# A banded convolution in windows of three quarters, with lent PSUM banks and shared copies, in front of a token-mixing kernel

## The chip, the cores and the metric

The kernel runs on one core of a Trainium2 chip. The metric is the device time in microseconds of one execution; a run's time is compared by the median of several. A profiled execution gives a trace of every instruction, with its span from the first instruction to the last.

## What is computed

The input `x` has 8 batches, 4224 tokens and 192 channels. A causal convolution with 7 taps runs over the tokens, with softmaxed weights per head (8 heads of 24 channels). Its result goes through a token mixing with phases. Cut to what matters:

```python
out = np.einsum('hk,bskhg->bshg', softmax(weight), windows_of_7(x))   # convolution
x = out
theta = x @ w_theta
zr, zi = x * np.cos(theta), x * np.sin(theta)
y = np.einsum('ts,bsd->btd', w_tok_r, zr) + np.einsum('ts,bsd->btd', w_tok_i, zi)
u = x + y
return u + np.maximum(u @ w_ch, 0.0)
```

The token mixing is by far the largest part: two 4224 x 4224 matrices, each against 8 x 192 columns.

## The kernel before

**Tiling.** The source tokens are cut into 33 chunks (`NCH`) of 128 tokens. A chunk is not contiguous: it has four quarters of 32 tokens (`NQ`, `Q`), one from each quarter of the sequence, and `tokens(c, a)` gives the first token of quarter `a`. The target tokens are cut into 17 units of two blocks of 128 tokens, of which the last has one block. A pair of blocks is done with seven products in place of eight (a Strassen-like scheme with the sums S1 to S4 of weight blocks and T1 to T4 of operands), each in two halves of the columns: 14 matmuls of 384 columns for each chunk and unit, at line 659.

**Visits.** A visit takes one unit through all chunks that are in SBUF at that time, at most 11 (`SLOTS`). `FIRST` says at which visit each of the first 11 chunks enters; every later chunk enters 17 visits after the chunk whose slot it takes. So the first visit works with one chunk, the second with two, and so on to eleven; at the end the number falls again. Between the visits to a unit its partial sums go to DRAM (`part`) and come back. Three of the smallest late visits are moved forward (`extra`), with small tiles of their own.

**A chunk's preparation** (`Chunk`, `prepare`). Each quarter of x is loaded to a buffer `xw` (cast to bf16 on the way), with its 16 history rows: for chunk 0 from DRAM, for the others by a DMA from the chunk before's `xw` (line 265, on SP). The convolution is a matmul with a band matrix `bands` as its stationary side: two quarters of 48 rows (96 rows) at a time, two accumulating matmuls for each head, 16 for each chunk (line 403). Two heads share a PSUM bank, and ScalarE copies each bank to `xz` (line 411). From there the chunk is stored to DRAM (`xs`, for the residual), and transposed: by TensorE with a VectorE copy to `uT` (line 443) for the first 11 chunks, by DMA for the later ones. Channel matmuls with `wth` (line 452) give angles, VectorE clamps them (line 320), ScalarE takes sines (line 348), and VectorE multiplies (line 357) and makes the T operands (line 369) in the chunk's slot tiles r0, i0, r1, i1, t1, t2, t4.

**Weights.** For each visit POOL issues loads of the two token matrices to `st` (line 485). VectorE transposes them in 32 x 32 blocks (line 507) and makes the sums S (line 521).

**PSUM.** Of eight banks, 0 to 5 take the products ("x", "y" and "s", two each). Only banks 6 and 7 serve convolution, transposes and channel matmuls. A product bank's partial result is copied by ScalarE to another bank (line 731) or starts a sum `d` (line 684), or is added to `d` by VectorE (line 686).

**Order.** Every instruction of the main part is a `Step`, with the engine, an assumed duration, its predecessors and the landing time of its DMA. A planner (`Schedule`) simulates the five engines with these assumptions, and issues each engine's instructions in the order that comes out: each engine and each DMA queue then follows this fixed order on the chip. `START` says when each engine is free after the set-up, `LAND` how long DMAs take.

**Set-up.** Before the planned part, POOL makes 0/1 masks, VectorE builds the band matrices (lines 857 to 873), and TensorE runs 18 matmuls on zeros (line 881) that use the identity as their stationary side.

Of the kernel before, what the change touches and what calls it, by code (L numbers as in the profile page):

```python
# [16 lines left out]
def kernel(  # L17
# [22 lines left out]
    nc = tc.nc  # L40
# [9 lines left out]
    HALO = 16  # L50
    WR = Q + HALO
    NT = S // P
    HN = N // 2
# [4 lines left out]
    FIRST = (0, 1, 2, 3, 4, 5, 6, 7, 8, 9, 10)  # L58
    CLAMP = 1.5
    EXTRA = 3  # L60
    BY_PE = 4
    SMALL = 3
# [73 lines left out]
    def pair(u):  # L136
        return 2 * u + 1 < NT


    def pair(u):  # L140
        return 2 * u + 1 < NT


# [22 lines left out]
    class Step:  # L166
        def __init__(self, engine, us, run, after=(), lands=0.0, wire=0.0, frees=None, mm=False):
            self.engine, self.us, self.run = engine, us, run
            self.after, self.lands, self.wire = list(after), lands, wire
            self.frees, self.mm = frees, mm  # L170
            self.due, self.want, self.fixed, self.end = None, None, None, None
            self.number = len(steps)
            steps.append(self)

# [20 lines left out]

    bands = constp.tile([2 * WR, 2 * H + 1, 2, Q], BF16, name="bands")
    nc.vector.memset(bands, 0.0)


    def channel_weights(w, name, after=()):  # L200
        R = D - P
        made = {}

        def clear():
            made["t"] = t = wk.tile([P, 4, D], BF16, name=name, tag="wc", bufs=1)
            dve(nc.vector.memset(t[:, 1:3, :], 0.0))

        ready = [Step("dve", 0.25, clear, after)]
        for lo, hi, k, r0, r1 in ((0, P, 0, 0, P), (0, R, 1, P, D), (R, P, 2, 0, R), (0, P, 3, R, D)):
            ready.append(Step(  # L210
                "pool", 0.6, lambda lo=lo, hi=hi, k=k, r0=r0, r1=r1: pool(nc.gpsimd.dma_start(
                    out=made["t"][lo:hi, k, :], in_=w[r0:r1, :]
                )), ready[:1], lands=4.0, wire=0.3,
            ))
        return (lambda: made["t"]), ready

    xw = tiles(wk, 2, [2 * WR, 2, B, D], BF16, "xw")
    rings = {k: Ring(2) for k in ("xw", "xz", "uT", "ang", "xr", "st", "x", "y", "s")}
# [4 lines left out]
    def load_x(c, a, n, lo, t0, h, k):  # L223
        pool(nc.gpsimd.dma_start(  # L224
            out=xw[k][lo : lo + n, h, :, :],
            in_=x[:, t0 : t0 + n, :].rearrange("b s d -> s b d"),
        ))


    class Chunk:  # L230
        def __init__(self, c):
            self.c, self.early = c, c < SLOTS
            self.k, self.uses, prev = rings["xw"].take()
            self.loads = []
            for a in range(NQ):
                h, lo = a // 2, (a % 2) * WR
                t0 = tokens(c, a)
                if c or t0 == 0:
                    lo += HALO
                else:  # L240
                    t0 -= HALO
                n = (a % 2 + 1) * WR - lo
                args = (c, a, n, lo, t0, h, self.k)
                if c == 0:
                    if t0 == 0:
                        nc.vector.memset(xw[0][0:HALO, 0, :, :], 0.0)
                    load_x(*args)
                    s = Step("none", 0.0, None)
                    s.fixed = START["x0"]
                else:  # L250
                    s = Step(
                        "pool", 0.6, lambda args=args: load_x(*args), [prev],
                        lands=LAND["x"], wire=0.87,
                    )
                self.loads.append(s)
            self.uses += self.loads
            chunks[c] = self
            xwk = xw[self.k]
            self.filled = list(self.loads)
            if c:  # L260
                before = chunks[c - 1]

                def history(a):
                    h, lo = a // 2, (a % 2) * WR
                    sp(nc.sync.dma_start(
                        out=xwk[lo : lo + HALO, h, :, :],
                        in_=xw[before.k][lo + Q : lo + Q + HALO, h, :, :],
                    ))

                for a in range(NQ):  # L270
                    s = Step(
                        "sp", 0.6, lambda a=a: history(a), [before.loads, prev],
                        lands=LAND["history"], wire=0.15,
                    )
                    before.uses.append(s)
                    self.filled.append(s)
            self.uses += self.filled[NQ:]

        def prepare(self):
            c = self.c  # L280
            zk, self.xzuse, prev = rings["xz"].take()
            self.xz = xzt[zk]
            copies = []
            for hp in range(H // 2):
                m = Step("pe", 0.34, lambda b, hp=hp: self.conv(b, hp), [self.filled, bands_ready, prev], mm=True)
                self.uses.append(m)
                e = Step(
                    "act", 0.5, lambda b, hp=hp: self.conv_copy(b, hp), [m], frees=m
                )
                copies.append(e)  # L290
            self.xzuse += copies
            self.xf = self.xz[:, :, :].rearrange("p b d -> p (b d)")
            if c + 2 < NCH:
                Chunk(c + 2)
# [8 lines left out]
            for g in range(2):  # L303
# [3 lines left out]
                turned = transposed(src, uT, [copies, prev], self.early, "sp")  # L307
# [4 lines left out]
                for k2 in range(2):  # L312
# [3 lines left out]
                    )  # L316
                    uuse.append(m)
# [80 lines left out]
        def conv(self, b, hp):  # L398
            for hh in range(2):
                h = 2 * hp + hh  # L400
                for half in range(2):
                    at = 2 * h + 1 - half
                    pe(nc.tensor.matmul(  # L403
                        banks[b][:, hh * B * G : (hh + 1) * B * G],
                        lhsT=bands[:, at : at + 2, :, :].rearrange("p z a m -> p (z a m)"),
                        rhs=xw[self.k][:, half, :, h * G : (h + 1) * G],
                        start=(half == 0), stop=(half == 1),
                    ))

        def conv_copy(self, b, hp):  # L410
            act(nc.scalar.activation(  # L411
                out=self.xz[:, :, hp * 2 * G : (hp + 1) * 2 * G].rearrange(
                    "p b (h g) -> p h b g", h=2
                ),
                in_=banks[b][:, 0 : 2 * B * G].rearrange("p (h b g) -> p h b g", h=2, b=B),
                func=AT.Copy,
            ))

# [7 lines left out]
    def transposed(u, uT, after, by_pe, queue):  # L426
# [8 lines left out]
        def turn(b):  # L435
# [7 lines left out]
        e = Step("dve", 0.55, lambda b: dve(nc.vector.tensor_copy(  # L443
            out=got(uT).rearrange("p k s -> p (k s)"),
            in_=banks[b][:, :].bitcast(BF16)[:, 0 : 6 * P],
        )), [m], frees=m)
# [19 lines left out]
    class Weights:  # L466
# [89 lines left out]
        def tile(self, name):  # L556
            t = self.tiles[name]
            return small_tile()[:, t] if self.small else t
# [7 lines left out]
    def freed_xw():  # L566
        return [s for u in rings["xw"].uses[-2:] for s in u]


    def small_tile():  # L570
        big_tile()
        if "small" not in late:
            late["small"] = wk.tile([P, 7, SMALL, NQ, Q], BF16, name="small", tag="xw")
        return late["small"]

    def big_tile():
        if "big" not in late:
            late["big"] = wk.tile([P, 2, HN], F32, name="late", tag="xw")
        return late["big"]
# [5 lines left out]
    def container(k):  # L585
        if ("u", k) not in late:
            if k < 4:
                both = wk.tile([P, 2, HN], BF16, name="ubT", tag=("ang", "xz")[k % 2])
# [10 lines left out]
    class Visit:  # L599
# [79 lines left out]
        def add(self, q, bank, g, after, begins=False, ends=False):  # L679
            def run():  # L680
                o = self.d[q]()[:, g * PC : (g + 1) * PC]
                y = banks[bank][:, 0:PC]
                if self.first and begins:
                    act(nc.scalar.activation(out=o, in_=y, func=AT.Copy))  # L684
                else:
                    dve(nc.vector.tensor_tensor(out=o, in0=y, in1=o, op=ALU.add))  # L686

            if self.first and begins:
                s = Step("act", 0.49, run, [after, self.start[q]])
# [14 lines left out]
        def products(self):  # L704
# [4 lines left out]
            for r in "xys" if self.pair else "xy":  # L709
                for g in gs:  # L710
                    k, uses[r, g], prev[r, g] = rings[r].take()
                    rows[r, g] = 2 * "xys".index(r) + k

# [15 lines left out]
            def copy(g):  # L729
                kx, ky = rows["x", g], rows["y", g]  # L730
                s = Step("act", 0.48, lambda: act(nc.scalar.activation(  # L731
                    out=banks[ky][:, 0:PC], in_=banks[kx][:, 0:PC], func=AT.Copy
                )), [at["x", g], prev["y", g]])
# [39 lines left out]
        def output(self, q):  # L773
            k, use, prev = outring.take()
            if len(outring.uses) <= 5:
                prev = [
                    s for r in ("ang", "xz", "uT") for u in rings[r].uses[-2:] for s in u
# [37 lines left out]
    START = {"x0": 8.0, "pe": 12.3, "dve": 12.3, "act": 6.3, "pool": 6.6, "sp": 2.0}  # L815
    LAND = {
        "x": 9.0, "history": 6.0, "keep": 6.0, "turn": 11.0, "w": 8.0, "d": 7.5, "store": 5.5,
        "xr": 7.0, "out": 5.0,
    }
    EARLY, SLACK = {}, 12.0  # L820
    noise = wk.tile([P, 512], BF16, name="noise", tag="ang")
    nc.vector.memset(noise, 0.0)
    Chunk(0)
    masks = wk.tile([2 * WR, KS, 2, Q], BF16, name="masks", tag="ang")
# [240 lines left out]
```

## Time and profile before

| | before |
|---|---|
| median of 10 runs | 1443.54 us (1438.73 to 1454.54) |
| the profiled execution | 1442.13 us |
| its span, first instruction to last | 1440.1 us |
| TensorE busy, share of the span | 98% |
| VectorE busy | 77% |
| ScalarE busy | 23% |
| GpSimd (POOL) busy | 36% |
| mean granted TensorE clock | 0.996 |

The time of an execution is 2 us longer than its span. Lines in the profile stand for source lines of the kernel. Busy times of TensorE are modelled from pipelined instructions, so the duration of one matmul in a group overlaps with the next; the distance between two is read from the chain of waits.

### The profile page before, as it was taken

What the parts mean: (1) busy time and instruction counts of PE and PEld (TensorE: products, weight loads), DVE (VectorE), ACT (ScalarE), POOL (GpSimd) and SP (SyncE); (2) the same over time, 40 slices, a digit from 0 to 9 for tenths busy, and PEclk for the clock granted to TensorE, in tenths of its full rate; (3) what the DMA queues carried; (4) which work ended last, traced back from release to release, by engine and by line L of the source; (5) the groups of instructions that cost most, each with busy time, mean ns of one, the idle gap of its engine ahead of it and who ended that gap; (6) DMA issues with size and microseconds to landing.
All of it is one profiled execution on the core that took longest, in us unless ns stands there. A gap on an engine that the chain in (4) does not pass through costs nothing.

```text
span 1440.1 us, 24960 instructions
## 1 busy us (share of the span) xinstructions
PE 1408.6 (98%) x9486; PEld 895.5 (62%) x9486; DVE 1102.8 (77%) x1835; ACT 335.7 (23%) x582; POOL 513.4 (36%) x778
## 2 busy tenths in 40 slices
PE   6899999999999999999999999999999999999997
PEld 3666666666666666666666666666666665666665
DVE  7998764446778987885576888788886878787788
ACT  5764422122212212210000221222121211211221
POOL 7543321124234552133134445225553354411120
PEclk8999999999999999999999999999999999999999
DMA  9999883679999999988799999999995999999994
GB/s 131 257 222 209 155 164 93 123 132 239 198 222 228 253 238 215 223 205 198 183 203 191 234 251 236 220 217 221 248 267 116 212 267 217 237 233 215 237 226 154
DMA packets 341351, 298.44 MB, mean 207 GB/s; under 512 B 160784, under 2 KB 287760, under 8 KB 341232
## 3 DMA queue, kind: packets, MB, share of 16 engines
q0 software_dynamic: 171072, 97.81, 50.6%
q1 hardware_dynamic: 130160, 189.21, 42.7%
q10 hardware_dynamic: 40000, 9.84, 5.4%
q8 instruction: 74, 1.21, 0.3%
q14 instruction: 45, 0.37, 0.1%
HBM read 250.21 MB, written 106.56 MB: 248 GB/s over the span
## 4 chain that ended last, share of the span: by engine, by line
PE 89%; DMA 4%; DVE 2%; issue 1%; ACT 1%; DVEq 0%; SPq 0%; ACTq 0%
PE bank L659 81%; PE bank L452 5%; DMA ubT<-ubT 4%; PE bank L403 3%; PE bank L438 1%; DVE d L686 1%; DVE w L521 0%; DVE d L799 0%; DVE w L507 0%; DMA xw<-xw 0%; DVE ubT L443 0%; ACT ubT L780 0%; DVE uT L443 0%; DVE ang L320 0%; ACT i L348 0%
## 5 line engine op out<-in xcount | busy, mean ns | idle before, releaser
L659 PEld LDWEIGHTS <-w 128*128 128x128 bf16 x7572 | 736.6, 98 | 466.4 <-issue 5.2
L659 PE MATMUL bank<-t,w 128*128 128x384 bf16 x3198 | 558.4, 327 | 1.6 <-DVE w L521 1.4
L686 DVE TENSOR_TENSOR d<-bank,d 128x384 f32<-128x384 f32 x542 | 291.6, 548 | 185.3 <-PE bank L659 156.7
L659 PE MATMUL bank<-i,w 128*128 128x384 bf16 x2220 | 396.3, 327 | 1.0 <-ACT bank L731 0.7
L507 DVE STREAM_TRANSPOSE w<-st 128x640 bf16<-128x640 bf16 (+5 forms) x416 | 340.4, 846 | 70.1 <-PE bank L659 63.0
L659 PE MATMUL bank<-r,w 128*128 128x384 bf16 x2154 | 384.1, 326 | 1.4 <-DVE r L357 1.2
L485 POOL DMA_DIRECT2D st<-in_moe_w_tok_r_dram x244 | 139.9, 582 | 400.7 <-DVE w L507 348.1
L485 POOL DMA_DIRECT2D st<-in_moe_w_tok_i_dram x244 | 139.3, 579 | 150.6 <-DVE w L507 139.5
L521 DVE TENSOR_TENSOR w<-w 128x1408 bf16<-128x1408 bf16 (+10 forms) x220 | 178.2, 810 | 2.5
L631 POOL TENSOR_TENSOR d<-d,xr 128x768 f32<-128x768 f32 x62 | 107.9, 1741 | 147.6 <-DMA xr<-xs 103.0
L224 POOL DMA_DIRECT2D xw<-in_x_dram x132 | 76.4, 588 | 154.9 <-PE bank L403 129.7
L348 ACT ACTIVATE r<-ang,half_pi 128x768 bf16<-128x768 f32 x44 | 41.1, 933 | 311.3 <-DVE ang L320 311.2
L731 ACT ACTIVATE bank<-bank 128x384 f32<-128x384 f32 x116 | 55.0, 477 | 215.8 <-PE bank L659 195.4
L684 ACT ACTIVATE d<-bank 128x384 f32<-128x384 f32 x132 | 63.3, 491 | 160.3 <-PE bank L659 158.6
L411 ACT ACTIVATE xz<-bank 128x384 bf16<-128x384 f32 x132 | 60.4, 489 | 168.4 <-issue 115.4
L320 DVE TENSOR_SCALAR ang<-bank 128x384 f32<-128x384 f32 x132 | 68.7, 550 | 25.8 <-PE bank L452 25.1
L799 DVE SCALAR_TENSOR_TENSOR d<-bank,d 128x384 f32<-128x384 f32 x106 | 55.3, 550 | 20.1 <-PE bank L452 19.5
L780 ACT ACTIVATE ubT<-d 128x768 bf16<-128x768 f32 x44 | 36.8, 842 | 144.5 <-DVE d L686 114.9
L452 PEld LDWEIGHTS <-uT 128*128 128x128 bf16 x632 | 55.6, 98 | 18.4 <-issue 3.4
L403 PE MATMUL bank<-xw,bands 96*128 96x192 bf16 x528 | 60.0, 247 | 2.0 <-ACT xz L411 1.1
L452 PE MATMUL bank<-wth,uT 128*128 128x192 bf16 x528 | 59.1, 249 | 2.6 <-DMA wth<-in_moe_w_theta_dram 1.7
L403 PEld LDWEIGHTS <-bands 96*128 96x128 bf16 x528 | 46.9, 98 | 15.4 <-issue 3.8
(68 smaller groups left out, 551.0 us busy)
## 6 DMA issues: line engine op xcount, KB each, us to landing
part<-d SPq DMA_DIRECT2D x172, 384.0 KB, 4.3
d<-part SPq DMA_DIRECT2D x159, 384.0 KB, 5.3
st<-in_moe_w_tok_r_dram POOLq DMA_DIRECT2D x152, 176.0 KB, 6.4
st<-in_moe_w_tok_i_dram POOLq DMA_DIRECT2D x152, 176.0 KB, 7.3
out_dram<-d SPq DMA_DIRECT2D x53, 384.0 KB, 6.5
xs<-xz SPq DMA_DIRECT2D x132, 96.0 KB, 5.0
xr<-xs POOLq DMA_DIRECT2D x66, 192.0 KB, 7.2
xw<-in_x_dram POOLq DMA_DIRECT2D x129, 96.0 KB, 5.8
```

The lines of the kernel that those rows point to most:

```text
L224: pool(nc.gpsimd.dma_start(out=xw[k][lo : lo + n, h, :, :], in_=x[:, t0 : t0 + n, :].rearrange("b s d -> s b d"),))
L320: "dve", 0.55, lambda b, k2=k2, g=g: dve(nc.vector.tensor_scalar(out=self.ang[g][:, k2 * 2 * D : (k2 + 1) * 2 * D], in0=banks[b][:, 0 : 2 ...
L403: pe(nc.tensor.matmul(banks[b][:, hh * B * G : (hh + 1) * B * G], lhsT=bands[:, at : at + 2, :, :].rearrange("p z a m -> p (z a m)"), rhs= ...
L411: act(nc.scalar.activation(out=self.xz[:, :, hp * 2 * G : (hp + 1) * 2 * G].rearrange("p b (h g) -> p h b g", h=2), in_=banks[b][:, 0 : 2 ...
L452: pe(nc.tensor.matmul(banks[bk][:, b * D : (b + 1) * D], lhsT=tT[:, 3 * k + b + i, :], rhs=w[:, 2 * b + i, :], start=(i == 0), stop=(i == ...
L485: "pool", 0.58, lambda a=a, t0=t0, i=i, w=w: pool(nc.gpsimd.dma_start(out=st[i][a * Q : (a + 1) * Q, 0:nb, 0 : n * Q], in_=w[r0 : r0 + nb ...
L507: lambda c=c, ce=ce: dve(nc.vector.transpose(self.tile(name)[:, c:ce, :, :], st[i][:, at : at + NQ, c * Q : ce * Q].rearrange("p bt (c j) ...
L521: s = Step("dve", 0.15 + 0.069 * n, lambda: dve(nc.vector.tensor_tensor(out=flat(self.tile(name)), in0=flat(self.tile(p)), in1=flat(self.t ...
L631: a = Step("pool", 1.75, lambda: pool(nc.gpsimd.tensor_tensor(out=tile_(), in0=tile_(), in1=xrt[k], op=ALU.add)), [r, s])
L659: pe(nc.tensor.matmul(banks[bank][:, 0:PC], lhsT=self.w.block(a, c), rhs=chunks[c].operand(b, g), start=(start and c == self.lo), stop=(c ...
L684: act(nc.scalar.activation(out=o, in_=y, func=AT.Copy))
L686: dve(nc.vector.tensor_tensor(out=o, in0=y, in1=o, op=ALU.add))
```

## The change

Convolution. A unit of work is now a `Window` of three quarters (`WQ`), whatever chunks they belong to: window m takes quarters 3m to 3m + 2, counted through all chunks. Each quarter has its own 6 halo rows in front of it (`ROWS` is 38, `WR` is 114). One matmul for each head and window convolves all three, so that nothing is accumulated. The band matrix is stored with a zero block between, so that the slice `at : at + NQ` puts a quarter on the output rows where its chunk has it. Halo rows come from DRAM for the first two windows, and later by DMA from the window in SBUF that holds the quarter's predecessor. There are three `xw` and three `xz` buffers in place of two. A bank now holds rows of one or two chunks, and is copied by one or two instructions: one for each chunk, and two where a chunk's part of more than one quarter starts at an odd quarter.

Copies. `copy_step` makes a step that the planner can give to ScalarE or, where `either` is set, to VectorE: the convolution's copies of the first four chunks, the evictions of the first four visits that start a sum or copy a bank, and all copies of transposes.

Banks. The first two windows' convolutions, and the transposes and channel matmuls of chunk 0, use banks 2 to 5 ("lent"), before the first visit takes these; two matmuls initialise the y banks.

Entry. `FIRST` is now (0, 0, 1, ..., 9): chunks 0 and 1 enter in visit 0. Since later chunks follow theirs by 17 visits, chunks 11 and 12 enter together in visit 17, and 22 and 23 in visit 34. There are 60 visits in place of 61.

Set-up. POOL issues the loads of two windows (11 DMAs, in groups around the masks) and of `wth` before those of the first weights. The taps' terms are made by one multiplication and added as a tree. The 24 matmuls on zeros use the zeros as their stationary side too, and need no identity.

```diff
-    WR = Q + HALO
+    WQ = 3
+    ROWS = Q + KS - 1
+    WR = WQ * ROWS
-    FIRST = (0, 1, 2, 3, 4, 5, 6, 7, 8, 9, 10)
+    FIRST = (0, 0, 1, 2, 3, 4, 5, 6, 7, 8, 9)
+    EITHER, TURNED = 4, 11
...
+    def copy_step(o, i, after, us, frees=None, either=False):
+        def run(*b):
+            if s.engine == "dve":
+                dve(nc.vector.tensor_copy(out=o(), in_=i(*b)))
+            else:
+                act(nc.scalar.activation(out=o(), in_=i(*b), func=AT.Copy))
+        s = Step("act", us, run, after, frees=frees)
+        s.also = "dve" if either else None
+        return s
...
+    bands = constp.tile([WR, H, NQ + WQ, Q], BF16, name="bands")
+    nc.vector.memset(bands[:, :, WQ, :], 0.0)
...
+    xw = tiles(wk, 3, [P, B, D], BF16, "xw", bufs=3)
+    rings.update({k: Ring(3) for k in ("xw", "xz")})
...
+        def halo(self, j, lo, prev):
+            m, i = divmod(self.m * WQ + j - NQ, WQ)
+            w, last_row = windows[m], (i + 1) * ROWS
+            s = Step("sp", 0.55, lambda: sp(nc.sync.dma_start(
+                out=xw[self.k][lo : lo + KS - 1, :, :],
+                in_=xw[w.k][last_row - KS + 1 : last_row, :, :],
+            )), [prev, w.rows[i]], lands=LAND["halo"], wire=0.1)
...
+            for c, quarters in into.items():
+                lo, hi = quarters[0], quarters[-1] + 1
+                if lo % 2 and hi - lo > 1:
+                    copies.append((c, lo, lo + 1))
+                    lo += 1
+                copies.append((c, lo, hi))
+            at = -a0 % NQ
+            def conv(b, hp):
+                for hh in range(2):
+                    h = 2 * hp + hh
+                    pe(nc.tensor.matmul(
+                        banks[b][:, hh * B * G : (hh + 1) * B * G],
+                        lhsT=bands[:, h, at : at + NQ, :].rearrange("p z m -> p (z m)"),
+                        rhs=xw[self.k][0:WR, :, h * G : (h + 1) * G],
+                        start=True, stop=True,
+                    ))
...
-        for _ in range(3):
-            pe(nc.tensor.matmul(banks[k], lhsT=ident, rhs=noise, start=True, stop=True))
+        for _ in range(4):
+            pe(nc.tensor.matmul(banks[k], lhsT=noise[:, 0:P], rhs=noise, start=True, stop=True))
```

The functions that used `xw` and `xz` late in the kernel (`freed_xw`, `small_tile`, `big_tile`, `container`) take their tiles from the new rings, and the planner knows steps of two engines, the second set of banks, and that DMAs of the first 30 us land in half the time (`CALM`).

## The prediction

> **What bounds the kernel now.** I read the page's engine rows, then engine busy time by stage, then the chain of waits for the price of one matmul, then the groups that the change touches.
>
> ```profile
> PE 1408.6 (98%) x9486; PEld 895.5 (62%) x9486; DVE 1102.8 (77%) x1835; ACT 335.7 (23%) x582; POOL 513.4 (36%) x778
> 0.00:100.00 100.00, 84.02 (x608) 53.92 (x609) 86.27 (x190) 60.91 (x117) 59.37 (x117) 0.95 1.12 202
> 100.00:1100.00 1000.00, 1000.00 (x6595) 630.23 (x6594) 745.21 (x1156) 208.46 (x372) 359.98 (x524) 1.00 0.94 204
> 1100.00:1420.00 320.00, 311.96 (x2169) 202.32 (x2168) 256.00 (x460) 63.16 (x91) 94.07 (x138) 1.00 1.12 219
> 1420.00:1440.00 20.00, 12.60 (x120) 9.04 (x117) 15.32 (x31) 3.15 (x4) 0.00 (x0) 0.99 0.58 195
> ...
> 40.00:60.00 20.00, 17.76 (x146) 12.21 (x147) 19.57 (x42) 15.28 (x30) 12.23 (x22) 1.00 1.21 256
> ```
>
> Columns of a stage: length, then PE, weight load, VectorE, ScalarE and GpSimd busy time, granted clock, DMA share, GB/s. From 100 to 1100 us TensorE is never idle: there a removed matmul is worth its whole time, and nothing else is worth anything. In the first 100 us VectorE is the fullest engine (19.57 of 20 us in the last row), ScalarE next.
>
> ```profile
> 48.53 0.33 PE bank L403 x4
> 1120.65 0.66 PE bank L452 x8
> 1121.31 11.70 PE bank L659 x72
> ...
> L403 PE MATMUL bank<-xw,bands 96*128 96x192 bf16 x528 | 60.0, 247 | 2.0 <-ACT xz L411 1.1
> L411 ACT ACTIVATE xz<-bank 128x384 bf16<-128x384 f32 x132 | 60.4, 489 | 168.4 <-issue 115.4
> ```
>
> The chain gives the pitch, which the mean of one (247 ns) hides: 83 ns for a 192-column matmul, with 96 rows (L403) as with 128 (L452), and 163 ns for a 384-column product. So useful TensorE work is 7656 products x 0.1628 + 528 convolution and 1056 channel matmuls x 0.0825 + 228 transposes x 0.0555 = 1389.7 us, and 50.4 of the 1440.1 us of span are lost. Where: I call lag the clock minus the useful work done. By 100 us, 282 products, 224 of the 192-column matmuls and 84 transposes are done, 69.1 us, so the lag is 30.9. It stays there to 1100, grows by 9.7 up to 1420 (waits for `ubT<-ubT` DMA transposes, 1.9 and 2.8 us the longest) and by 11 in the last 20 us.
>
> **The change part by part.** The sum is made against the profiled execution, 1442.1 us for a span of 1440.1; the median of the runs is 1.4 above it.
>
> *Fewer convolution matmuls.* 33 chunks of 4 quarters, three at a time, are 44 windows x 8 heads = 352 matmuls for 528. The rows grow from 96 to 114; the pitches above show that rows cost nothing. 176 x 0.0825 = 14.5 us less, minus two matmuls that initialise the y banks (0.3): **-14.2**. The six added noise matmuls lie before the first convolution.
>
> *The ramp.* Here the saving can be lost, because VectorE sets the pace. Chunks 0 to 5 get their last VectorE operand (line 369) at 25.9, 38.5, 50.2, 63.3, 77.5 and 94.6 us. The work behind that: per chunk 4 angles x 0.50, 4 products x 0.555, 4 differences x 0.555, 2 transposed copies x 0.50; per visit 4 adds x 0.55 and weights of 1.4 + 0.78n us (n chunks): 11.0 + 0.78n, or 12.6 at n = 2 and 14.1 at n = 4, as measured. One fewer visit drops its adds, weights and ten ScalarE evictions, but each remaining visit has one more chunk to fetch weights for, and VectorE gets new work. I counted both VectorE orders up to chunk 5's last operand at these prices: 78.8 us after, 80.1 before. Of the 25 uT copies that it makes now, 9 stay with it, and 8 xz, 6 d and 3 bank copies come (17 x 0.48 = 8 us).
> VectorE starts earlier: its first xz copy follows the first convolution, about 12.3 us, where its first copy now comes at 15.3. But with one visit fewer TensorE has done less by then. VectorE's clock minus TensorE's useful work, at the operand of each visit where it is largest (prices x 0.96, which fits the measured times): before 28.4 (fifth visit, T1), after 30.4 (T1 of chunk 4). Before, the real lag was 2.5 above this count. After, I add 2.5 and 1.0 for a later weight: POOL issues the first `st` load at 6.65 us now, and after it has been put behind eleven x loads and the four of `wth`, at some 12; VectorE then reaches its first transpose at about 17.5 us, a load issued by 14 lands near 18. Ramp lag 33.9 for 30.9: **+3.0**. The bounds: -3, if ScalarE's help removes what the count can't see, and +10, if ScalarE becomes a second pace. Its copies of the convolution grow from 132 to 308, 300 of them on ScalarE, since a window's three quarters mostly fall in two chunks. No row shows a 32-row copy; a 16-row memset (xw, 768 elements, 0.70 us) beside a 96-row one (bands, 544, 0.51) says that elements per row set the price, so a piece costs a whole one's 0.49. ScalarE's count to chunk 4's last sine rises from 45.2 to 52.7 us, about 65 on the clock, where VectorE needs it near 70: 5 us of cover.
>
> *Clock.* In the trace the grant is 1.00 to 16 us, then 0.50 until about 26, though TensorE never stood for long:
>
> ```profile
> 14.00:16.00 2.00, 1.16 (x14) 0.81 (x13) 0.72 (x2) 0.67 (x2) 2.00 (x5) 1.00 1.16 142
> 18.00:20.00 2.00, 1.99 (x12) 1.61 (x12) 1.45 (x4) 0.35 (x1) 1.86 (x4) 0.50 1.20 191
> ```
>
> The Trainium skill's "TensorE: Matmul & The Clock Gate" (Part 1) says that an idle window of some 3.4 us halves the clock and as long a busy one restores it. That speaks against the change: the noise matmuls no longer wait for the identity (6.75 us now), so 24 of them run from 1.9 to about 8.6 us (my estimate from the 5.35 us of 18) and leave 3 us of idleness before the bands. By the rule the first 16 convolutions, 12 transposes and half the channel matmuls, 2.7 us of work, would run at half speed, +2.7. By the trace that stage is paced by copies, and the cold stretch was there anyway: +0. I take **+0.5**.
>
> *Band set-up.* Replaced by one 1792-element multiply; between 1.8 (by the `w` sums' rate, 1408 elements in about 1.1 us, plus its broadcast) and 2.9 us (7 x 0.42, the rows of L862), with less after it: bands at 11.3 to 12.9 us, 12.2 before. Zero; it is inside the range's ramp bounds.
>
> *Two chunks entering together at visits 17 and 34.* T3 and T1 of a late chunk can be written only after visit 16's last use of r1 (352.6 us) and are read some 12 us later; one chunk had both by 359.7. Two need 2 x 2 x 0.57 = 2.3 us on VectorE instead of 1.1. 0 to 2 us each: **+0.5** for both.
>
> *Tail.* Transposed copies on either engine: about four of 0.55 us in the last 20 us, half of them on the chain's VectorE at most: **-0.5**. *One visit fewer* also drops 4 stores and 4 loads of 384 KB of 298 MB, and halos shrink from 16 to 6 rows; SP and DMA hide them beside products. If POOL's or SP's order makes a load late, the cover is VectorE's 25% idle time of the middle stage. *Third xw/xz buffers, late tiles waiting for xz too*: TensorE has no wait on xz after 140 us; zero.
>
> Sum: -14.2 + 3.0 + 0.5 + 0.5 - 0.5 = -10.7; 1442.1 becomes 1431.4, the median 1443.5 becomes 1432.8.
>
> **The rivals.**
> A (forecast, 0.50): as above, 1427 to 1438.
> B, the ramp improves (0.20): earlier first products (chunk 0 no longer waits for `wth` up to 18 us) and shared copies take the lag to 28. For it: ScalarE had 39% idle. Against: the VectorE count. -14.2 - 3 - 0.5 = 1426; range 1419 to 1430.
> C, the ramp eats it (0.17): the 5 us of ScalarE cover are gone, ScalarE and VectorE wait for each other in fixed orders, lag 41: -14.2 + 10 + 1 = 1440; range 1436 to 1448. For it: 300 copies for 132 ahead of sines on an in-order queue.
> D, slower (0.13): bank holding. Only banks 6 and 7 serve convolution, transposes and channel matmuls after the start. Each is now held for two ScalarE copies in turn (0.98 us for 0.49) for half as much TensorE work, in 132 of 176 fillings. If the next user waits 0.17 us each time, 132 x 0.17 = 22 us and the kernel is 8 us slower, 1451; it decides from 0.16 us on. For it: TensorE already waits for `xz L411` (1.1 us, three times). Against: all of these lie before 75 us, and up to 30 us of products stand between fillings later.
> That the count of matmuls doesn't fall is excluded: the new TensorE order holds 352.
>
> **How the numbers follow.** Half a per cent (7.2 us) is about what a measurement tells from no change. Below 1436.3 lie 0.45 of A, B's 0.20 and 0.04 of C: 0.69. Above 1450.8 lies D and a trace of C: 0.13. Between: 0.18. A range of 1421 to 1447 leaves out D and the best of B.
>
> **What would show it.** Convolution group x352 with 83 ns pitch in the chain; TensorE idle-free from 110 to 1100 us; VectorE at 19 of 20 us until about 80; lag at 110 us near 34. Wrong if TensorE waits on xz copies after 150 us (D), if ScalarE is fuller than VectorE from 30 to 80 us (C), if lag at 110 is under 30 (B).

## The result, and the profile after

The median after the change is 1431.87 us (15 runs, 1426.83 to 1444.86); the runs of the kernel before that stood beside it and beside the experiments have a median of 1442.8 us (50 runs, 1436.7 to 1454.54). The ratio is 0.9926 [0.9907, 0.9946]: the change takes off 10.9 us, where 10.7 were forecast. The profiled execution took 1427.44 us, its span is 1425.7 us. Executions of one and the same kernel are up to 18 us apart here; where that comes from is part of what follows.

First the engine rows of the page of the changed kernel:

```profile
PE 1400.1 (98%) x9318; PEld 884.7 (62%) x9318; DVE 1101.9 (77%) x1803; ACT 429.4 (30%) x761; POOL 511.2 (36%) x779
```

ScalarE has 94 us more to do (335.7 before), VectorE and POOL as much as before, TensorE 168 instructions fewer. Next busy time by stage, with the columns of the prediction's table (length, then PE, weight load, VectorE, ScalarE, GpSimd, granted clock, DMA share, GB/s):

```profile
0.00:100.00 100.00, 84.56 (x553) 51.99 (x554) 85.36 (x175) 73.29 (x136) 60.44 (x121) 0.91 1.02 173
100.00:1100.00 1000.00, 1000.00 (x6534) 625.91 (x6532) 752.34 (x1161) 285.80 (x526) 355.96 (x521) 1.00 0.94 200
1100.00:1406.00 306.00, 302.86 (x2115) 197.68 (x2114) 250.50 (x443) 67.17 (x96) 94.82 (x138) 1.00 1.14 229
1406.00:1426.00 20.00, 12.64 (x123) 9.16 (x121) 13.71 (x27) 3.12 (x4) 0.00 (x0) 0.94 0.53 171
...
40.00:60.00 20.00, 16.93 (x129) 10.67 (x129) 19.27 (x43) 17.89 (x33) 10.85 (x20) 1.00 1.22 239
```

TensorE is still never idle from 100 to 1100 us. From 40 to 60 us VectorE is as full as before (19.27 of 20 us), but ScalarE is now beside it with 17.89, where it had 15.28.

Then the chain of waits and the convolution's group:

```profile
346.49 0.33 PE bank L323 x4
349.92 9.75 PE bank L721 x60
...
L323 PE MATMUL bank<-xw,bands 114*128 114x192 bf16 x352 | 52.9, 250 | 7.3 <-DVE bands L953 3.6
L185 ACT ACTIVATE xz<-bank 32x384 bf16<-32x384 f32 (+2 forms) x300 | 139.4, 481 | 99.8 <-issue 58.6
```

Four convolution matmuls take 0.33 us, 83 ns each, with 114 rows as with 96; 352 are left of 528. The 60 products beside them stand at 162.5 ns each. ScalarE makes 300 copies to `xz`, and their mean of 481 ns is that of the 128-row copies before (489): by form, 127 of 32 rows take 478 ns, 131 of 64 and 42 of 96 rows 482. Rows don't set the price of a copy.

The lag (the clock minus the useful work of TensorE, at the pitches of the prediction), read off the matmuls of the traces, shows where the two kernels part:

| lag at, us | 20 | 40 | 60 | 80 | 100 | 1100 | 1200 | 1300 | 1400 | end | useful | span |
|---|---|---|---|---|---|---|---|---|---|---|---|---|
| before | 16.8 | 25.2 | 29.0 | 30.5 | 30.9 | 29.6 | 33.7 | 38.4 | 39.1 | 50.3 | 1389.7 | 1440.1 |
| after | 16.9 | 28.8 | 34.4 | 36.3 | 37.7 | 36.3 | 40.2 | 40.3 | 40.1 | 50.3 | 1375.4 | 1425.7 |

Useful work falls by 14.3 us. The first 100 us lose 6.8 us more than before, 5.3 of it between 20 and 60 us, and the time after 1100 us gives 6.7 back: in these two executions the lags end level. (The small fall of the lag from 100 to 1100 us says that the pitches are taken about a thousandth too high.)

### The profile page after: what moved, and what is told of

The parts are those of the page before. It is cut to its first block, busy times and chain, and to the rows that moved or that the text cites. A ratio compares the mean times of both kernels' runs of the same rounds, so it can differ in the third digit from the quotient of the medians.

```text
span 1425.7 us, 24789 instructions
## 1 busy us (share of the span) xinstructions
PE 1400.1 (98%) x9318; PEld 884.7 (62%) x9318; DVE 1101.9 (77%) x1803; ACT 429.4 (30%) x761; POOL 511.2 (36%) x779
## 4 chain that ended last, share of the span: by engine, by line
PE 91%; DVE 3%; POOL 2%; issue 2%; DMA 2%; ACT 0%; DVEq 0%; POOLq 0%; ACTq 0%
PE bank L721 83%; PE bank L509 5%; PE bank L323 2%; DMA st<-in_moe_w_tok_r_dram 1%; PE bank L494 1%; POOL xw L277 1%; DVE w L564 1%; DVE d L874 1%; DMA xr<-xs 1%; POOL st L542 1%; DVE d L745 1%; DVE ang L397 0%; DVE w L578 0%; POOL d L693 0%; DVE r L434 0%
## 5 line engine op out<-in xcount | busy, mean ns | idle before, releaser
L745 DVE TENSOR_TENSOR d<-bank,d 128x384 f32<-128x384 f32 x532 | 287.7, 548 | 173.9 <-PE bank L721 144.4
L721 PE MATMUL bank<-r,w 128*128 128x384 bf16 x2154 | 392.2, 326 | 1.4 <-DVE r L434 0.8
L564 DVE STREAM_TRANSPOSE w<-st 128x640 bf16<-128x640 bf16 (+4 forms) x412 | 343.0, 855 | 65.1 <-PE bank L721 56.6
L721 PE MATMUL bank<-i,w 128*128 128x384 bf16 x2220 | 390.0, 327 | 1.6 <-DVE bank L183 1.3
L578 DVE TENSOR_TENSOR w<-w 128x1408 bf16<-128x1408 bf16 (+9 forms) x216 | 186.5, 863 | 2.4
L185 ACT ACTIVATE xz<-bank 32x384 bf16<-32x384 f32 (+2 forms) x300 | 139.4, 481 | 99.8 <-issue 58.6
L693 POOL TENSOR_TENSOR d<-d,xr 128x768 f32<-128x768 f32 x61 | 103.8, 1702 | 90.5 <-DMA xr<-xs 39.3
L874 DVE SCALAR_TENSOR_TENSOR d<-bank,d 128x384 f32<-128x384 f32 x106 | 54.5, 548 | 12.7 <-PE bank L509 10.9
L323 PE MATMUL bank<-xw,bands 114*128 114x192 bf16 x352 | 52.9, 250 | 7.3 <-DVE bands L953 3.6
L425 ACT ACTIVATE i<-ang 128x768 bf16<-128x768 f32 x66 | 54.7, 829 | 8.1 <-PE bank L721 8.1
```

What stands on the lines that cost most here:

```text
L185: act(nc.scalar.activation(out=o(), in_=i(*b), func=AT.Copy))
L323: pe(nc.tensor.matmul(banks[b][:, hh * B * G : (hh + 1) * B * G], lhsT=bands[:, h, at : at + NQ, :].rearrange("p z m -> p (z m)"), rhs=xw[ ...
L425: act(nc.scalar.activation(out=z, in_=self.ang[g], func=AT.Sin, **({"bias": half_pi[:], "scale": 1.0} if i == 0 else {}),))
L564: lambda c=c, ce=ce: dve(nc.vector.transpose(self.tile(name)[:, c:ce, :, :], st[i][:, at : at + NQ, c * Q : ce * Q].rearrange("p bt (c j) ...
L578: s = Step("dve", 0.15 + 0.069 * n, lambda: dve(nc.vector.tensor_tensor(out=flat(self.tile(name)), in0=flat(self.tile(p)), in1=flat(self.t ...
L693: a = Step("pool", 1.75, lambda: pool(nc.gpsimd.tensor_tensor(out=tile_(), in0=tile_(), in1=xrt[k], op=ALU.add)), [r, s])
```

## The experiments

Three questions: is a removed matmul worth its time; what made the start lag twice as much as counted; and is the gain at the end real, and whose is it. Every edit is to the changed kernel where nothing else is said. A ratio is to the kernel before, so that 0.9926 stands for "as the changed kernel".

**Is the saving worth its time? `e1_528`.**

```diff
+                    if hh == 0:
+                        pe(nc.tensor.matmul(banks[b][:, 0 : B * G], ..., start=True, stop=True))
                     pe(nc.tensor.matmul(
                         banks[b][:, hh * B * G : (hh + 1) * B * G],
```

The first of each two convolution matmuls is issued twice, so that there are 528 again, and nothing else changes.

> The changed kernel with the first of each two convolution matmuls issued twice into the same place, so that 528 are issued again in place of 352; order and all else unchanged. If a convolution matmul is worth its whole pitch where TensorE never idles, and the start is paced by other engines, the cost is 176 x 0.0825 = 14.5 us less what falls before 100 us (7 to 9 of the 44 windows, some 28 to 36 of the 176 matmuls, 2.3 to 3 us): 11.5 to 14.5 us over the changed kernel, about 1445. If the saving was hidden by waits anyway, under 5 us. In the profile the lag at 100 us (clock less useful work, with the repeats counted as useful) falls by up to 3 us from 37.7.

Median 1441.57 us, ratio 0.9994 [0.9963, 1.0024]. Useful work is 1389.9 us, and the span of its profile 1439.8 us, 14.1 longer than after's, with a lag of 37.0 at 100 us and 49.9 at the end (37.7 and 50.3). The added rows stand beside the old ones:

```profile
L323 PE MATMUL bank<-xw,bands 114*128 114x192 bf16 x352 | 68.8, 254 | 7.1 <-DVE bands L960 3.7 <-ACT xz L185 2.0 <-DVE ang L404 1.2
L330 PE MATMUL bank<-xw,bands 114*128 114x192 bf16 x176 | 44.3, 252 | 0.0
```

Between profiles the matmuls are worth their whole time; between medians they are worth 9.7 us. That is less than the 11.5 to 14.5 expected; the 14.5 us of the count still lie within what the two intervals allow together, but the medians leave room for less.

**The start: the clock. `e2_noise7`.**

```diff
-        for _ in range(4):
+        for _ in range(7):
             pe(nc.tensor.matmul(banks[k], lhsT=noise[:, 0:P], rhs=noise, start=True, stop=True))
```

42 matmuls on zeros in place of 24 bridge the time in which TensorE waits for the bands.

> The changed kernel with 42 matmuls on zeros ahead of the first convolution in place of 24, so that TensorE is busy until about 12.7 us and not until 9.4. If the cold stretches of the start cost time through TensorE (the Trainium skill's rule on an idle window), the grant stays at 1.00 past 14 us and the kernel is 1.5 to 2.7 us faster. If the first 20 us are paced by copies and by landings, as my prediction took it, 0 to 0.7 us. If the 42 run past the bands, they delay the first convolution by less than 1 us.

Stretches of 2 us, of after first:

```profile
10.00:12.00 2.00, 0.00 (x0) 0.00 (x0) 1.28 (x3) 0.00 (x0) 2.00 (x8) 1.00 0.73 70
...
14.00:16.00 2.00, 1.49 (x9) 0.99 (x7) 1.90 (x5) 1.29 (x4) 1.99 (x5) 0.51 0.68 58
16.00:18.00 2.00, 1.63 (x14) 1.36 (x15) 1.42 (x3) 1.30 (x4) 2.00 (x5) 0.50 1.10 187
```

and of `e2_noise7`:

```profile
14.00:16.00 2.00, 1.03 (x9) 0.60 (x7) 1.97 (x5) 1.36 (x4) 1.99 (x5) 1.00 0.67 57
16.00:18.00 2.00, 1.53 (x19) 1.24 (x20) 1.29 (x3) 1.77 (x4) 2.00 (x5) 1.00 1.17 207
```

After's TensorE stands still from 10 to 12 us and is granted half the clock from 14 to 21 us; with the bridge it keeps the full clock there, and does five more matmuls from 16 to 18 us with less busy time. Both fall to half again from 24 to 31 us, and after a third time, from 34 to 38 us. The lag at 100 us is 35.9. Five traces with after's order in the start (after, `e9_again`, `e5_after_turn16`, `e11_turn8`, `e12_bype9`) have 37.7, 37.2, 38.0, 38.0 and 38.2: the half clock that the bridge takes away costs 1.3 to 2.3 us. The medians don't show it: 1434.89 us, 0.9931 [0.9904, 0.9957].

**The start: the set-up. `e10_setup`.** The creation of each of the first two windows is moved one place down, so that POOL makes the masks behind two loads of window 0 and most of the block ahead of window 1's loads; there are 30 matmuls on zeros.

```diff
-    Window()
     masks = wk.tile([WR, KS, WQ, Q], BF16, name="masks", tag="ang")
...
     Window()
     block = constp.tile([WR, WQ], F32, name="block")
...
+    Window()
-        for _ in range(4):
+        for _ in range(5):
```

> The changed kernel with POOL's set-up in another order: masks ahead of most of the first window's loads, block ahead of the second window's, and 30 matmuls on zeros for 24. VectorE now waits 1.6 us for the masks and 0.8 us for block, so the bands come at some 11 us, not 13.2, and TensorE's idle gap before them goes. If the first convolution and the cold clock after the gap cost the ramp (1.4 and 1.7 us by the changed kernel's profile and the run with 42 matmuls), lag at 100 us falls by 1.5 to 3 us, and the time to about 1430. If the second window's loads (landing near 13 us) or the first weights hold VectorE anyway, under 1 us.

VectorE in order of time (start, duration, instruction, and in brackets the idle time before it and what ended it), of after and then of `e10_setup`:

```profile
7.34 0.28 DVE L934 TENSOR_TENSOR taps<-masks 114x224 bf16<-114x224 bf16 x1 [1.63 <-POOL masks L902]
12.13 1.03 DVE L953 TENSOR_SCALAR bands<-terms,block 114x512 bf16<-114x512 bf16 x3 [0.77 <-POOL block L911]
...
18.69 0.56 DVE L397 TENSOR_SCALAR ang<-bank 128x384 f32<-128x384 f32 x1 [0.92 <-PE bank L509]
20.45 0.43 DVE L564 STREAM_TRANSPOSE w<-st 128x256 bf16<-128x256 bf16 x1
```

```profile
9.68 0.88 DVE L953 TENSOR_SCALAR bands<-terms,block 114x512 bf16<-114x512 bf16 x3
14.61 1.52 DVE L183 CAST xz<-bank 32x384 bf16<-32x384 f32 x3 [2.60 <-PE bank L323]
```

After's bands end at 13.16 us: VectorE waits 1.63 us for the masks and 0.77 for the block, which POOL makes behind loads. The edit brings them to 10.56 us, and then VectorE waits 2.60 us for the convolution of window 1, whose loads come that much later. Lag at 100 us 37.9, time 1431.73 us, 0.9922 [0.9894, 0.9949]: as after. But the edit puts one wait in place of another: VectorE's first transpose of weights comes at 20.23 us, 0.22 earlier than in after. So what earlier bands are worth by themselves stays untested; this way of getting them gains nothing.

**The start: who paces it? `e4_either0`, `e8_nolent`.**

```diff
-    EITHER, TURNED = 4, 11
+    EITHER, TURNED = 0, 11
```

> The changed kernel with EITHER 0: copies of the convolution and evictions that start a sum or copy a bank all stay on ScalarE (transposes' copies remain free to choose). If VectorE alone sets the ramp's pace, my count of its work takes the lag down by up to 7 us (22.8 for 29.9 at the S1 of the fourth visit), and the kernel is 3 to 7 us faster. If ScalarE is as near to the pace as VectorE (17.9 and 17.6 of 20 us busy from 40 to 80 us now, over 19 then), it is 0 to 5 us slower, with lag over 38 at 100 us.

This gives the shared copies of convolution and evictions back to ScalarE. My VectorE count falls by 7 us, and the lag rises instead: 41.9 at 100 us, and a time of 1437.41 us, 0.9955 [0.993, 0.998]. The stretch from 40 to 80 us, of after and then of `e4_either0`:

```profile
40.00:80.00 40.00, 36.19 (x262) 22.29 (x262) 38.04 (x80) 35.46 (x67) 21.15 (x38) 1.00 1.20 233
```

```profile
40.00:80.00 40.00, 33.19 (x238) 20.47 (x237) 32.51 (x65) 32.59 (x65) 18.57 (x33) 0.99 1.06 206
...
PE bank L721 <- ACT bank L185: 3.5, 4, 1.5
PE bank L494 <- ACT xz L185: 3.2, 3, 1.7
```

VectorE has 7.5 us of idle time there, and TensorE's longest waits from 12 to 100 us (total, times, longest), but for that for the bands (3.8 us), end on ScalarE's copies. With the sharing, VectorE is full and ScalarE is 35.46 of 40 us busy. So both pace the start, and a count of one engine cannot give the lag.

`e8_nolent` sets `lent` to `False` in its three places, so that the first two windows and chunk 0 use banks 6 and 7 like all others.

```diff
-                m.lent = self.m < 2
+                m.lent = False
```

> The changed kernel without lent banks: the first windows' convolutions and chunk 0's transposes and channel matmuls go through banks 6 and 7 like all others. If the first copies are held up by two banks, the first product comes 1 to 3 us later and the kernel is as much slower. If VectorE's start is set by other things (bands at 13.2 us, weights, wth), under 1 us.

Lag 41.1 at 100 us (+3.4), 1434.9 us, 0.9953 [0.9927, 0.9978]: the lent banks are worth some 3.5 us in the start.

Four of these edits and after can be put side by side by two instructions of VectorE, its first transpose of weights and the last operand of chunk 5 (start of the one, end of the other, in us):

| | first transpose of weights | chunk 5's last operand | lag at 100 us |
|---|---|---|---|
| after | 20.45 | 94.6 | 37.7 |
| `e2_noise7` | 19.42 | 92.9 | 35.9 |
| `e10_setup` | 20.23 | 94.9 | 37.9 |
| `e8_nolent` | 23.79 | 98.3 | 41.1 |
| `e4_either0` | 19.45 | 100.1 | 41.9 |

The rows of `e2_noise7` and of `e8_nolent`:

```profile
19.42 0.43 DVE L564 STREAM_TRANSPOSE w<-st 128x256 bf16<-128x256 bf16 x1
```

```profile
23.79 0.77 DVE L564 STREAM_TRANSPOSE w<-st 128x256 bf16<-128x256 bf16 x2
```

With the sharing in place, the lag moves with the first transpose: by -1.8 and +3.4 us for -1.0 and +3.3, and hardly at all in `e10_setup`. Without it (`e4_either0`) the time is lost later, between that instruction and chunk 5.

**The two chunks that enter together. `e3_first`, `e7_before_pair`.** One takes them out of the changed kernel, the other puts them into the kernel before.

```diff
-    FIRST = (0, 0, 1, 2, 3, 4, 5, 6, 7, 8, 9)
+    FIRST = (0, 1, 2, 3, 4, 5, 6, 7, 8, 9, 10)
```

> The changed kernel with the entry of before: FIRST is (0, 1, ..., 10), one chunk a visit, 61 visits. My count of VectorE's work against TensorE's puts the ramp's lag 2.1 us higher (32.5 for 30.4), while visits 17 and 34 take one chunk each: 0 to 3 us slower than the changed kernel, 1432 to 1435. The rival that the pair's entry is what cost the ramp 6.8 us: 3 to 7 us faster, with a lag of 31 to 34 at 100 us.

> The kernel before with the new entry alone: FIRST is (0, 0, 1, ..., 9), 60 visits, two chunks together. My count puts the ramp's lag 2 us lower (26.4 for 28.4); undoing it in the changed kernel cost 2.9 us of ramp and 11 us in all. If the entry alone is worth 2 to 3 us, 1440; if it also acts on the late stage whatever the convolution, 1430 to 1435; if two chunks in one visit need the other parts (banks, copies), no gain or slower.

| | lag at 80 | 100 | 1100 | 1300 | 1400 | end | ratio |
|---|---|---|---|---|---|---|---|
| `e3_first` (1443.56 us) | 40.0 | 40.5 | 40.5 | 50.5 | 53.9 | 64.2 | 0.9987 [0.9954, 1.0021] |
| `e7_before_pair` (1435.58 us) | 29.1 | 29.1 | 27.8 | 33.3 | 37.2 | 48.3 | 0.9961 [0.9936, 0.9985] |

The entry in one visit is worth 2.8 us of the lag at 100 us in the changed kernel and 1.8 in the one before (the count said 2.1 and 2). The ratios differ from those of after and before by 0.0061 and 0.0039, 8.8 and 5.6 us: by the medians another 4 to 6 us lie behind 1100 us. These differences are uncertain by 5.6 and 3.5 us, and the profiles don't show them: from 1100 to 1400 us `e3_first` loses 13.4 us, where two executions of the changed kernel lose 3.8 and 13.1, and `e7_before_pair` loses 9.4, before 9.5. Without it the changed kernel is at most 7 us faster than before and perhaps not faster at all. The later double entries cost nothing: after's lag is 37.2 and 37.3 at 340 and 380 us (visit 17), 36.8 and 36.7 at 700 and 780 us (visit 34).

**The end: how much of it is chance? `e9_again`, `e12_bype9`.** `e9_again` is the changed kernel without an edit.

> The changed kernel once more, unchanged, for a second profile of it. If the ramp is set by fixed orders and engine work, its lag at 100 us is within 0.5 us of 37.7 again; if what differs between runs (1427 to 1445 us) lies in the late stage, the growth from 1100 us to the last 20 us is another than 3.8 us, and carries the whole difference in time.

It took 1436.46 us, 9.0 more than the profiled execution above. At 100 us its lag is 37.2, at 1100 us 36.1, in the last part it loses 10.2 (10.2 after), but between 1100 and 1400 us it loses 13.1 where the other lost 3.8. TensorE's waits in this stretch, of `e9_again`, with a link of its chain:

```profile
PE bank L509 <- DMA ubT<-ubT: 4.8, 2, 3.6
PE bank L721 <- DVE d L745: 2.6, 1, 2.6
PEld L509 <- DMA ubT<-ubT: 6.2, 3, 4.0
...
1254.63 16.82 DMA ubT<-ubT
1271.50 1.46 PE bank L509 x8
```

In after only the second of these waits is there. The channel matmuls of finished blocks wait for a DMA transpose that took 16.82 us from issue to landing. From 1260 to 1280 us the lag grows by 6.6 us: TensorE stands for 4.8, and then has half the clock for 3.4 us. Another 1.6 us come behind the wait near 1186 us, which is equally long in both, 2.6 us: `e9_again` gets less of the clock there, and after does not. After first:

```profile
1184.00:1188.00 4.00, 2.28 (x15) 1.37 (x15) 2.90 (x5) 0.84 (x1) 1.18 (x1) 1.00 1.26 235
```

```profile
1184.00:1188.00 4.00, 2.20 (x8) 1.02 (x8) 2.61 (x4) 0.84 (x1) 0.00 (x0) 0.71 1.29 194
```

`BY_PE` says how many of the last blocks are transposed by TensorE instead:

```diff
-    BY_PE = 4
+    BY_PE = 9
```

> The changed kernel with BY_PE 9 in place of 4: the outputs of the last nine visits, not four, are transposed by TensorE, so that 20 DMA transposes go and 120 TensorE transposes come, 120 x 0.0555 = 6.7 us of useful work. If the waits that differ from run to run (1265 to 1356 us in the profiles, ubT<-ubT at channel matmuls) are these DMA transposes, the lag grows by under 1 us after 1220 us, only the wait near 1186 us stays, the spread of the runs narrows to about half, and the median is 0 to 4 us above the changed kernel's, since 3 to 7 us of waits pay for the 6.7. If the waits only move to d tiles and weights, the kernel is 6 to 9 us slower.

This puts 120 transposes, 6.7 us, on TensorE and takes 20 DMA transposes away. The time is 1435.01 us, 0.9942 [0.9921, 0.9963]: slower than after by 2.3 us by the ratios, a third of the work put in, though the intervals overlap. Its 6 runs lie between 1434.54 and 1437.99 us, 3.5 us apart where the changed kernel's are 18 apart. From 1220 us on TensorE has no wait left to speak of, and the waits from 1100 to 1406 us are short:

```profile
1220.00:1410.00 190.00, 189.59 (x1408) 126.46 (x1407) 154.88 (x274) 52.22 (x74) 48.86 (x74) 1.00 0.85 196
...
PE bank L721 <- DVE d L745: 2.0, 1, 2.0
PE bank L509 <- DMA ubT<-ubT: 0.4, 1, 0.4
```

So most of the difference between executions is late DMA transposes, with the half clock behind them; the rest is the clock behind the other wait, and small waits. What stays is the wait near 1186 us, which after has as well. Its chain there:

```profile
1163.04 8.38 DMA xr<-xs
1172.26 11.86 DMA st<-in_moe_w_tok_r_dram
1185.15 0.53 DVE d L745
```

A load of weights, issued behind a load of the residual, lands 11.86 us later.

**The end: the planner's assumption. `e5_after_turn16`, `e6_before_turn16`, `e11_turn8`.** `LAND` takes 11 us for a DMA transpose. 16 in the changed kernel, 16 in the kernel before, and 8 in the changed kernel:

```diff
-        "x": 9.0, "halo": 5.5, "keep": 6.0, "turn": 11.0, "w": 8.0, "d": 7.5, "store": 5.5,
+        "x": 9.0, "halo": 5.5, "keep": 6.0, "turn": 16.0, "w": 8.0, "d": 7.5, "store": 5.5,
```

> The changed kernel with the planner told that a DMA transpose lands after 16 us, not 11 (only the fixed orders change). In the profiles after 1100 us TensorE waits for late transposes; lag grows by 3.8 us there in the changed kernel's profile and by 9.6 in the kernel before's, while their runs spread over 15 us. If these landings are what differs between runs, and what gave the change the 3 us that my ramp left out, the late growth falls under 2 us, the spread narrows, and the median falls by 2 to 5 us, to 1427 to 1430. If the late wait is VectorE's or the weights' (2.8 us at 1186 us in the profile, for a d sum), nothing changes within 2 us, or it is slower, as channel matmuls come later.

> The kernel before with the same assumption of 16 us. If late transposes cost it 7 to 9 us, it becomes 5 to 8 us faster (1435 to 1438), and the distance to the changed kernel with 16 us is what matmuls and ramp leave: 14.2 - 6.7 = 7.5 us. If they don't, it stays at 1443.

> The changed kernel with the planner told that DMA transposes land after 8 us. With 16 us both kernels became 8 to 10 us slower. If the late stage is set by how long an output holds its d tile (the plan keeps tiles longer with 16), 8 us gives them back sooner: 0 to 4 us faster, late growth under 4 us. If late transposes themselves are what TensorE waits for, it now waits for them up to 3 us each more often: 3 to 8 us slower, with waits on ubT<-ubT at the channel matmuls.

All three are slower than the kernel that they edit: 1442.59 us, 0.9997 [0.9975, 1.0018]; 1450.78 us, 1.0072 [1.0052, 1.0093]; 1441.6 us, 0.9997 [0.9973, 1.002], each by some 10 us. Longer due times were expected to help, and did not. A link of the chain of `e5_after_turn16`:

```profile
1244.22 4.91 ACTq L488
1257.82 20.04 DMA ubT<-ubT
```

This transpose landed after 20.04 us, so that even 16 was short. With 8 the lag already grows from 38.0 at 100 us to 43.1 at 1100 us; channel matmuls wait for a chunk transposed by DMA, up to 388 us. The entry is not one duration: a change of it makes another order of everything, and these runs don't say which part of the order costs the 10 us.

No kernel here beats the changed one: the lowest ratio, 0.9922 of `e10_setup`, is the same within the intervals.

## Why the prediction was right, and where only by cancelling

The sum said -10.7 us, the medians say -10.9. Its terms, against the traces; the stage from 1100 to 1400 us is what the medians leave when useful work, the lag at 1100 us and the last part are taken from the profiles (10.3 us before, 8.3 after), so the column adds up to the medians by construction. The interval of the ratio is 2.8 us to either side, and the -2.0 is not told from zero:

| step | predicted | measured |
|---|---|---|
| fewer convolution matmuls | -14.2 | -14.3 |
| start (ramp +3.0, clock +0.5) | +3.5 | +6.7 (36.3 for 29.6 at 1100 us) |
| two chunks entering at visits 17 and 34 | +0.5 | 0 |
| tail | -0.5 | -1.0 (10.2 for 11.2 from 1400 us) |
| 1100 to 1400 us | not in the sum | -2.0 |
| time outside the span | not in the sum | -0.3 |
| sum | -10.7 | -10.9 |

*Fewer matmuls: right*, by count and by pitch, and shown by putting them back.

*The ramp: the mechanism half right, the size half of what it was.* The step that failed is the term on top of VectorE's count, a fixed 2.5 us and 1.0 for a later weight: the lag at 100 us is 7.3 us above the count (37.7 for 30.4), not 3.5. Before it was 2.5. The entry is not where the rest comes from: the lag stands above the count by 2.5 us in the kernel before and by 2.7 with the new entry in it (`e7_before_pair`, count 26.4), by 7.3 us in the changed kernel and by 8.0 with the old entry in it (`e3_first`, count 32.5). It comes with the other parts of the change: windows, set-up, copies and banks.

Much of it is there early. The bands were ready at 13.16 us, forecast for 11.3 to 12.9. VectorE was to start at 12.3 us and to reach its first transpose of weights at 17.5; it started at 13.60 and got there at 20.45, behind three angles of chunk 0, ahead of which VectorE waits for TensorE's channel matmuls for 0.92 and 0.15 us. With the 1.0 us that was allowed, that is 2 us late, of 3.2 us missing, and `e2_noise7` and `e8_nolent`, which move this instruction, move the lag with it. Last operands of chunks 0, 1 and 5 were ready at 27.5, 41.5 and 94.6 us, before at 25.9, 38.5 and 94.6. After and then before, from 12 to 40 us:

```profile
12.00:40.00 28.00, 20.73 (x118) 13.79 (x119) 23.22 (x50) 19.04 (x34) 18.81 (x37) 0.70 0.88 105
```

```profile
12.00:40.00 28.00, 22.40 (x148) 13.45 (x147) 22.24 (x54) 18.52 (x38) 18.11 (x33) 0.82 1.14 180
```

VectorE, called the pace, stands for 4.8 of 28 us, and stood for 5.8 before: it is not idle for longer, it has more to do by then (23.22 us for 22.24), and TensorE, for which it waits, has less of the clock. After's waits from 12 to 100 us give the partners:

```profile
PE bank L323 <- DVE bands L953: 3.6, 1, 3.6
PE bank L323 <- ACT xz L185: 2.1, 1, 2.1
```

The first is the late bands; the second is window 2's convolution, which waits for ScalarE's copies of a bank at 24.7 us. Late bands, clock and hand-overs between three engines are what these rows show; only the clock's part was measured by itself, and how the rest divides stays open.

*The clock: the rule pointed the right way.* The Trainium skill's "TensorE: Matmul & The Clock Gate" (Part 1) was given 2.7 us, the trace 0, the sum 0.5. The grant did fall to half 2 us earlier than before, behind a gap of 3.6 us. What the bridge took away is worth 1.3 to 2.3 us, between the two. That is not yet the difference to the kernel before, which has a stretch at half clock of its own: from 12 to 40 us the mean grant is 0.82 before, 0.70 after and 0.88 with the bridge. In proportion, about two thirds of those 1.3 to 2.3 us are the change's, 0.9 to 1.5 (my estimate from these three grants).

*The double entry: zero.* One visit less may also help in the end, which I did not count: the medians of `e3_first` and `e7_before_pair` point to it from both sides, 4 to 6 us behind 1100 us, and their profiles don't show it. Why it would is only argued: one small visit less and 3.1 MB less of stores and loads beside the late transposes.

*The rivals.* B fell: the lag rose. C was half right: ScalarE became a second pace at once (17.89 of 20 us, though not fuller than VectorE with 19.27, which was to be its sign), but its price stopped at about 7 us, not 10, since the sharing worked (`e4_either0` is C without it, lag 41.9). D fell: TensorE has no idle time from 110 to 1100 us, and its only wait of note on an `xz` copy, 2.1 us, lies in the start. A second ScalarE copy per bank hides behind products.

So the forecast of the time came so near by luck, through errors that offset each other: the start was put 3.2 us too low, and 2.0 us of gain at the end (if it is one) and 1.3 of small ones (double entry, tail, time outside the span) were not in the sum. Without the gains the kernel would have come out 3 us slower, still in the forecast's range of 1427 to 1438. The pair of profiled spans (-14.4 us) flatters the change, because this execution of after lost only 3.8 us between 1100 and 1400 us, where the median implies 8.3.

## What to carry to other kernels

Where an engine is idle-free for most of the span, the count of removed instructions times their pitch (from the chain, not from the mean) gives the gain, and all the doubt lies in the start and the end. In a start where three engines hand work to each other, count each engine, and add the hand-overs: here the lag stood 2.5 us above the fullest one's count in one kernel and 7.3 in the other. Before explaining a few us between two single profiles, find the stage in which the same kernel differs from itself.

## What the hardware showed that was not expected

- Small DMA transposes (`ubT<-ubT`) landed 2.8 us after their issue at best, 10.1 in the median and 15.9 at worst in the kernel before, and single ones took 16.8 us in `e9_again` and 20.0 in `e5_after_turn16`. They go with most of the spread between executions: without 20 of them it went from 18 to 3.5 us (over 15 and 6 runs).
- VectorE copies a bf16 bank to SBUF in 558 ns, ScalarE needs 811 for the same shape, where a 128x384 float32 bank costs ScalarE 0.47 to 0.49 us and VectorE about 0.55:

```profile
L185 ACT ACTIVATE uT<-bank 128x768 bf16<-128x768 bf16 x16 | 12.8, 811 | 8.5 <-PE bank L494 8.3
L183 DVE COPY uT<-bank 128x768 bf16<-128x768 bf16 x9 | 5.0, 558 | 7.0 <-PE bank L494 6.8
```

- The granted clock also falls without a long gap: before, it went to 0.50 at 16 us, though TensorE had been busy for 1.67 and 1.16 us in the two stretches of 2 us ahead of that, and had stood for 0.62 us at most. Nor does it always fall behind the same wait, as the two rows from 1184 to 1188 us show.
